# Two blocks of a weight matrix, fetched and converted among the first batch's squares

## The chip, the cores and the metric

The kernel runs on one core of a Trainium2 chip. The metric is the time of one execution in microseconds (us) of device time; lower is better. The engines named below are TensorE (PE, matrix products; PEld are its weight loads), VectorE (DVE), ScalarE (ACT), GpSimd (POOL) and SyncE (SP, which issues the DMA transfers). Each engine has its own sequence of instructions, written by the program, and waits where an operand isn't there yet.

## The reference

An attention over channels, followed by a gated two-layer network on all 24,320 tokens:

```
B, N, C = 4, 6080, 256;  d_ff = 2048
qn = q / (norm of q over the N tokens + 1e-6);  kn the same of k
s  = kn^T @ qn / tau              # [B, 256, 256]
a  = exp(s - s.max(-1));  a /= a.sum(-1) + 1e-9
x  = v @ a                        # [B, N, 256]
h  = x @ w_in                     # [B*N, 2048]
g  = h * sigmoid(1.702 * h)
out = g @ w_out                   # [B*N, 256]
```

q, k and v are float32; w_in and w_out are float64.

## The kernel before, in words

**What is computed where.** For each batch the kernel sums k^T q over the tokens into a 256 x 256 score matrix (TensorE), sums the squares of q and k for the norms, makes the softmax, and then folds the attention matrix into w_in: h = v @ (a @ w_in), so that the large work is one product of v with folded weights, a gate, and a product with w_out. The large products are done with operands split into a high and a low part (three matrix products for one), and by a seven-product scheme for 2 x 2 blocks (m1 to m7 in the listing). From about 71 us to the end TensorE does nothing but these; the loops there run over 4 batches, 6 chunks of tokens each, and 8 pairs of blocks of d_ff in each chunk.

**The float64 weights.** A block of w_in has 128 rows and 512 columns of float64 (512 KB). `win_fetch` loads it as pairs of 32-bit words, and `to_float32` makes float32 of it in two ScalarE steps (L132, L134) and four VectorE steps (L136, L138, L142, L147). `win_part` (L555, ScalarE) and `win_part_low` (L558, VectorE) then split the result into a high and a low part. The first two blocks (c = 0 and 1) make up the first group of columns; the first products of the folded weights (`weights_pair`, L602, tile ps_w) need both.

**The first batch.** `start_up` writes the instructions of the first batch's scores in program order. The 6080 tokens come in 25 units: units 0 to 23 are two groups of 128 tokens (the last of them one), unit 24 is the rest. For each unit `prepare` loads q and k, if the unit begins a load (units 1, 4, 7, 10, 13, 16, 19 begin one of 768 KB for q and one for k), squares both on ScalarE (L290, tile squares) and adds the squares to two running sums on VectorE (L293). `score` puts the unit's products on TensorE (L346, tile s), seven units behind `prepare`; a product of 128 x 256 stands in the trace as two passes. `add_both` (L298, L299) adds the two sums together. Behind the last unit stand, on SP's queue, the loads of w_in's first two blocks, w_out's first part, tau, v, and q and k of the next batch.

**The stretch that is planned.** What follows, to the end of the first 8 pairs, is put in order by `together`: it collects the instructions with estimated durations, and `arrange` places them engine by engine, with ready times for what is loaded or summed earlier (`late_at`; the token "acc" stands for the sum of squares). TensorE's row has a fixed order: the scores of units 18, 19 and 20, then `first_norms` (L451, tile ps_n, which needs the finished sum of squares), the scores of units 21 and 22, `first_spread` (L478, ps_b, which needs the norms' reciprocals from VectorE, L465 to L469, and diag from ScalarE), the scores of units 23 and 24, the transposes (L522), the folded weights (L602), then m5, m1, ... of the first pair (L719). Sixteen products for the next batch's scores (`score_first`, also L346) may be put between these from where the row stands at the transposes. ScalarE and VectorE get their order from the planner, so an instruction there that comes early can hold up what stands behind it.

The two blocks of w_in are among the planned work, behind the last square:

```
for c in range(NC2):
    state = win_convert(c, c)
    ...
    add("ACT", 0.62, ("win", 0, 0, c, 0), [("cv", "in", c, 5)], A.win_part, 0, c)
    add("DVE", 0.69, ("win", 0, 0, c, 1), [("win", 0, 0, c, 0)], A.win_part_low, c)
```

Of the kernel before, what the change touches and what calls it, by code (L numbers as in the profile page):

```python
# [28 lines left out]
def channel_attention_then_glu(  # L29
# [26 lines left out]
    NC2 = C // P  # L56
# [24 lines left out]
    cv = ctx.enter_context(tc.tile_pool(name="cv", bufs=2))  # L81
# [5 lines left out]
    def bank(tag, name):  # L87
        pool = {"a": ps_h, "b": ps_h, "c": ps_h, "s": ps_s}.get(tag, ps_o)
        return pool.tile([P, NCH], F32, tag=tag, name=name)
# [26 lines left out]
    def load_words(src, shape, pool=cv, tag="words"):  # L116
        raw = pool.tile([*shape, 2], U32, tag=tag, name="words")
        nc.sync.dma_start(raw, src)
        return raw
# [34 lines left out]
    win = {}  # L154

    def win_fetch(n):


        g, c = divmod(n, NC2)
        gs = slice(2 * g * GW, 2 * (g + 1) * GW)  # L160
        src = w_in[c * P : (c + 1) * P, gs].rearrange("p (f w) -> p f w", w=2)
        if g == 0:
            room = (sp, ("qs", "ks")[c])
        else:
            room = (wp, f"{('wh', 'wl')[c]}{g}")
        words["in", n] = load_words(src, [P, GW], *room)

    def win_convert(n, room=0):
        g, c = divmod(n, NC2)
        win[n] = sp.tile([P, GW], F32, tag=("raw_q", "raw_k")[c], name="win")  # L170
        yield from to_float32(win[n], words.pop(("in", n)), [P, GW], room)

    def wout_fetch(u):

        rows = w_out[2 * u * P : 2 * (u + 1) * P, :]
        src = rows.rearrange("(f p) (d w) -> p f d w", p=P, w=2)
        words["out", u] = load_words(src, [P, 2, C])
# [636 lines left out]
    def keep_warm():  # L814

        wide = gp.tile([P, NCH], F32, tag="g", name="wide", bufs=2)
        nc.vector.memset(wide, 1.0)
        ps = bank("b", "ps_y")
        for rhs in [ones] * 4 + [wide]:
            nc.tensor.matmul(ps[:, : rhs.shape[1]], lhsT=ones, rhs=rhs, start=True, stop=True)  # L820
# [3 lines left out]
    at, nxt = ats[:2]  # L824
# [2 lines left out]
    ready = []  # L827
    PAIRS = NF // 2

    def start_up():  # L830
        nc.scalar.activation(table, ones[:, 0:1], AF.Sqrt)
        keep_warm()
        for u in range(nu):
            ready.append(at.prepare(u))
            if u >= AHEAD:
                at.score(u - AHEAD, *ready[u - AHEAD])
        win_fetch(0)
        win_fetch(1)
        wout_fetch(0)
        nc.sync.dma_start(tau_sb, tau.partition_broadcast(P))  # L840
        v_load(0, 0, False)
        v_load(0, 0, True)
        nxt.fetched(0)
        nxt.fetched(2)
        win_fetch(2)
        win_fetch(3)
        at.add_both()
        wo.extend(wp.tile([P, NF, C], F32R, tag=f"wo_{n}", name=f"wo_{n}") for n in "hl")

    def first_softmax():  # L850

        A = at
        us = 1.0 / 0.68
        START = 36.4

        def add(eng, dur, token, deps, fn, *a):
            gather[0].append(Node(eng, dur * us, token, deps, fn, a))

        def score(u, *deps):
            dur = 0.86 if u == nu - 1 else 1.72  # L860
            add("PE", dur, ("s", u), deps, lambda: at.score(u, *ready[u]))

        def late_at(t, *tokens):
            for token in tokens:
                done(token, (t - START) * us)

        late_at(40.2, "acc")
        late_at(34.7, ("cv", "in", 0, "load"))
        late_at(36.0, ("cv", "in", 1, "load"))
        late_at(37.3, ("cv", "out", 0, "load"))  # L870
        late_at(41.5, "v1")
        late_at(44.8, "v2")
        late_at(47.5, ("raw", 1, 0))
        late_at(50.0, ("raw", 1, 1))
        late_at(51.4, ("cv", "in", 2, "load"))
        late_at(52.7, ("cv", "in", 3, "load"))
        add("SP", 0, ("cv", "out", 1, "load"), ["ns"], wout_fetch, 1)
        gather[0][-1].wait = 20.0

        s1 = nxt.score_first((2, 4, 6, 8, 10, 12, 14))  # L880
        score(nu - 7)
        score(nu - 6)
        score(nu - 5)
        add("PE", 0.65, "ns", ["acc"], A.first_norms)
        score(nu - 4)
        score(nu - 3)
        add("PE", 0.45, "nb", ["diag"], A.first_spread)
        score(nu - 2)
        score(nu - 1)
        for i in range(NC2):  # L890
            add("PE", 0.3, ("t", i), [("e", i)], A.transposes, i)
        for q in range(2):
            have = ["aTh", *(("win", 0, 0, c, 1) for c in range(NC2))]
            add("PE", 1.1 - 0.1 * q, ("w", 0, 0, q, "h"), have, A.weights_pair, 0, q, (0, 4))
            add("PE", 0.48, ("w", 0, 0, q), ["aTl"], A.weights_pair, 0, q, (4, 6))
        for n in range(8):
            add("PE", 0.86, ("s1", n), [("raw", 1, n // 4)], lambda: next(s1, None))
            gather[0][-1].flex = True

        add("ACT", 0.25, "root", ["ns"], A.first_root)  # L900
        add("DVE", 0.7, "turn", ["root"], A.first_turn)
        add("ACT", 0.5, "diag", ["turn"], A.first_diag)
        add("ACT", 0.4, "rq", ["nb"], A.first_rq)
        add("ACT", 1.5, "exp", ["root"], A.exp_table)
        for i in range(NC2):
            add("DVE", 0.9, ("x", i), ["rq", ("s", nu - 1)], A.softmax_a, i)
            add("ACT", 0.7, ("e", i), [("x", i), "exp"], A.softmax_b, i)
        add("DVE", 0.3, "z", [("e", 1)], A.softmax_c)
        add("ACT", 1.5, "table", ["aTh"], A.gelu_table)
        add("ACT", 0.59, "aTh", [("t", 1)], A.turned)  # L910
        add("DVE", 0.69, "aTl", ["aTh"], A.turned_low)

        for c in range(NC2):
            state = win_convert(c, c)
            key = ("cv", "in", c)
            for n, (eng, dur) in enumerate((("ACT", 0.6), ("ACT", 0.6), ("DVE", 0.42), ("DVE", 0.42), ("DVE", 0.67), ("DVE", 0.67))):
                add(eng, dur, (*key, n), [(*key, n - 1 if n else "load")], lambda s=state: next(s, None))
            add("ACT", 0.62, ("win", 0, 0, c, 0), [("cv", "in", c, 5)], A.win_part, 0, c)
            add("DVE", 0.69, ("win", 0, 0, c, 1), [("win", 0, 0, c, 0)], A.win_part_low, c)
        add("SP", 0, None, [("win", 0, 0, c, 1) for c in range(NC2)], A.win_keep, 0)  # L920

        V = ("v", 0, 0)
        for n in range(2):
            add("DVE", 0.69, (*V, "+", n), ["v1"], v_sum, 0, 0, False, n)
        for n in range(3):
            have = ["v2"] if n < 2 else [(*V, "+", 2), (*V, "+", 3)]
            add("DVE", 0.69, (*V, "+", 2 + n), have, v_sum, 0, 0, True, n)
        for tag, n, da, dd, have in (
            ("py", 0, 0.62, 0.69, [(*V, "+", 0)]),
            ("px", 0, 0.62, 0.69, ["v1"]),  # L930
            ("py", 1, 0.62, 0.69, [(*V, "+", 1)]),
            ("px", 1, 0.62, 0.69, ["v1"]),
            ("pz", 0, 0.62, 0.69, [(*V, "+", 2 + n) for n in range(3)]),
            ("pz", 1, 0.62, 0.69, [(*V, "+", 2 + n) for n in range(3)]),
            ("pw", None, 0.62, 0.69, [(*V, "+", 2 + n) for n in range(3)]),
        ):
            token = (*V, tag if n is None else f"{tag}{n}")
            add("ACT", da, (*token, 0), have, v_part, 0, 0, tag, n, False)
            add("DVE", dd, token, [(*token, 0)], v_part, 0, 0, tag, n, True)
        weight_ops(0, 0, gather[0])  # L940
# [15 lines left out]
    def done(token, t):  # L956
        if token is not None:
            ends[token] = t
# [49 lines left out]
    def arrange(nodes, row, ahead, near):  # L1008
# [1 line left out]
        ends = dict(begun_ends)  # L1010
        row = list(row)
        clock = dict.fromkeys(("PE", "ACT", "POOL", "SP"), 0.0)
        clock["ACT"], clock["DVE"] = 3.0, 5.6
        open_to = {e: [] for e in clock}
        users = {}
        unmet = {}
# [39 lines left out]
        while undone:  # L1056
            best = None
            for e in clock:
                at = list(choices(e))
# [19 lines left out]
            _, t, x = best  # L1079
# [27 lines left out]
    def together(n):  # L1107

        nodes = []
        gather.append(nodes)  # L1110
        first_softmax()
        for p in range(n):
            lay(p)
# [548 lines left out]
    for b in range(B):  # L1662
# [4 lines left out]
        if b + 1 < B:  # L1667
            o = b * NCHUNK * PAIRS
            u, last_u = ats[b + 1].direct, len(ats[b + 1].units)
# [57 lines left out]
```

## Time and profile before

| what | value |
|---|---|
| time, median of 3 runs | 2158.22 us (2157.47 to 2158.90) |
| span of the profiled execution | 2156.0 us |
| its own time beside its span | the profile gives the span alone; the median is 2.2 us above it |
| PE busy | 2148.4 us, 100% |
| ACT busy | 1552.9 us, 72% |
| DVE busy | 1278.0 us, 59% |
| POOL busy | 437.2 us, 20% |
| data moved by DMA | 153.5 MB, mean 71 GB/s |

The span runs from the first to the last instruction that the profiler saw; all starts below are counted from its beginning. Busy shares are means over stages with different limits: in the first 35 us the DMA engines are full, in the following 35 VectorE is, and then TensorE to the end. The duration of one instruction is from its start to its end; instructions of one engine overlap a little at their ends, so what a further one costs is the distance from start to start, which is shorter.

### The profile page before, as it was taken

Reading aid. Unit: us, or ns where it says so; the run is one execution under the profiler, and the core shown is the slowest. Engines: PE = TensorE matmul, PEld = TensorE weight load, DVE = VectorE, ACT = ScalarE, POOL = GpSimd, SP = SyncE. Lnnn points to the kernel's source line nnn. Section 1 sums busy time; section 2 is a strip of 40 time slices with the busy share of each in tenths; the row PEclk is TensorE's granted clock in tenths of the full one; section 3 lists DMA queues with packets and bytes.
Section 4 is the critical chain, followed back from the end, with each engine's and each line's share of the span. In section 5 each row is a group of like instructions: output and inputs, shape, how many; then the busy total and the mean of one; then the engine's idle time right before and its main releaser. Section 6 shows DMA issues by size and latency. Waiting matters only on the chain.

```text
span 2156.0 us, 26555 instructions
## 1 busy us (share of the span) xinstructions
PE 2148.4 (100%) x9720; PEld 1793.6 (83%) x9720; DVE 1278.0 (59%) x1925; ACT 1552.9 (72%) x2753; POOL 437.2 (20%) x457
## 2 busy tenths in 40 slices
PE   9999999999999999999999999999999999999999
PEld 8888888888888888888888888888888888888887
DVE  7986656655556565664555666566555545545443
ACT  7987777766777777776777777777676666666665
POOL 0003333230113342231012233223111200100100
PEclk9999999999999999999999999999999999999999
DMA  9433222221122121221113222122111110110100
GB/s 373 142 106 95 69 69 79 67 71 40 59 97 70 60 87 59 75 77 40 39 63 104 69 69 74 54 87 66 40 67 50 59 40 20 59 40 20 57 20 19
DMA packets 73843, 153.50 MB, mean 71 GB/s; under 512 B 6896, under 2 KB 14576, under 8 KB 73712
## 3 DMA queue, kind: packets, MB, share of 16 engines
q1 hardware_dynamic: 73712, 151.81, 21.2%
q8 instruction: 76, 1.25, 0.2%
q14 instruction: 55, 0.45, 0.1%
HBM read 122.68 MB, written 29.10 MB: 70 GB/s over the span
## 4 chain that ended last, share of the span: by engine, by line
PE 96%; DMA 2%; DVE 1%; ACT 0%; SPq 0%; issue 0%; DVEq 0%; ACTq 0%
PE ps_o L795 48%; PE ps_x L719 24%; PE ps_z L719 12%; PE ps_y L719 6%; PE s L385 4%; PE ps_w L584 2%; DMA raw<-in_k 1%; PE ps_w L602 0%; DMA v_raw<-in_vT 0%; DMA raw_k<-in_k 0%; DVE vl L701 0%; DVE v_raw L684 0%; SPq L263 0%; ACT vh L703 0%; PE ps_n L412 0%
## 5 line engine op out<-in xcount | busy, mean ns | idle before, releaser
L795 PE MATMUL ps_o<-gh,wo_l 128*128 128x512 f32 (+1 forms) x1536 | 594.9, 387 | 0.0
L795 PE MATMUL ps_o<-gh,wo_h 128*128 128x512 f32 (+1 forms) x1536 | 594.7, 387 | 0.0
L795 PE MATMUL ps_o<-gl,wo_h 128*128 128x512 f32 (+1 forms) x1536 | 470.6, 387 | 0.0
L782 DVE TENSOR_TENSOR gl<-g,gh 128x512 fp32r<-128x512 f32 (+1 forms) x384 | 274.6, 754 | 155.1 <-ACT gh L778 155.0
L330 POOL TENSOR_TENSOR acc<-acc,sq 128x256 f32<-128x256 f32 x276 | 228.1, 832 | 593.9 <-ACT sq L318 583.1
L782 DVE TENSOR_TENSOR gl<-ps_y,gh 128x512 fp32r<-128x512 f32 (+1 forms) x192 | 131.8, 686 | 348.8 <-ACT gh L778 348.4
L795 PEld LDWEIGHTS ps_o<-gh,wo_h 128*128 128x128 f32 x1536 | 288.3, 188 | 57.6
L795 PEld LDWEIGHTS ps_o<-gh,wo_l 128*128 128x128 f32 x1536 | 288.3, 188 | 57.5
L795 PEld LDWEIGHTS ps_o<-gl,wo_h 128*128 128x128 f32 x1536 | 288.3, 188 | 57.4
L719 PE MATMUL ps_x<-vh,wh 128*128 128x512 f32 (+1 forms) x768 | 299.6, 390 | 0.5 <-ACT g L773 0.2
L719 PE MATMUL ps_x<-vl,wh 128*128 128x512 f32 (+1 forms) x768 | 298.0, 388 | 0.0
L719 PE MATMUL ps_x<-vh,wl 128*128 128x512 f32 (+1 forms) x768 | 297.4, 387 | 0.0
L684 POOL TENSOR_TENSOR v_raw<-v_raw 128x512 f32<-128x512 f32 (+1 forms) x110 | 162.9, 1489 | 520.0 <-DMA v_raw<-in_vT 463.9
L773 ACT ACTIVATE r<-r 128x512 f32<-128x512 f32 (+1 forms) x192 | 120.6, 628 | 169.9 <-DVE r L762 169.9
L753 ACT COPY r<-ps_x 128x512 f32<-128x512 f32 (+1 forms) x189 | 110.3, 584 | 168.8 <-PE ps_x L719 168.4
L778 ACT CAST gh<-g 128x512 fp32r<-128x512 f32 (+1 forms) x384 | 216.2, 612 | 0.1
L782 DVE TENSOR_TENSOR gl<-r,gh 128x512 fp32r<-128x512 f32 (+1 forms) x192 | 150.7, 785 | 61.6 <-ACT gh L778 58.4
L719 PEld LDWEIGHTS ps_x<-vh,wh 128*128 128x128 f32 x768 | 144.4, 188 | 29.3 <-ACT g L773 1.6
L719 PEld LDWEIGHTS ps_x<-vh,wl 128*128 128x128 f32 x768 | 144.1, 188 | 28.9
L719 PEld LDWEIGHTS ps_x<-vl,wh 128*128 128x128 f32 x768 | 144.5, 188 | 25.4
L753 ACT COPY r<-ps_z 128x512 f32<-128x512 f32 (+1 forms) x192 | 112.2, 584 | 71.6 <-PE ps_z L719 70.5
L403 DVE TENSOR_TENSOR sums<-sums,s 128x256 f32<-128x256 f32 x138 | 57.9, 420 | 160.4 <-PE s L385 157.9
(137 smaller groups left out, 3263.9 us busy)
## 6 DMA issues: line engine op xcount, KB each, us to landing
v_raw<-in_vT SPq DMA_DIRECT2D x80, 512.0 KB, 4.2
out_T<-osb SPq DMA_DIRECT2D x80, 256.0 KB, 2.0
raw_q<-in_q SPq DMA_DIRECT2D x74, 256.0 KB, 2.6
raw_k<-in_k SPq DMA_DIRECT2D x74, 256.0 KB, 2.7
win_h<-win_h SPq DMA_DIRECT2D x16, 512.0 KB, 3.3
win_l<-win_l SPq DMA_DIRECT2D x16, 512.0 KB, 4.2
v_raw<-in_vT SPq DMA_DIRECT2D x16, 480.0 KB, 3.7
words<-in_w_in SPq DMA_DIRECT2D x8, 512.0 KB, 5.2
```

What stands on the lines that cost most here:

```text
L330: nc.gpsimd.tensor_tensor(acc, acc, sq[:, j, :], op=ALU.add)
L385: nc.tensor.matmul(out, lhsT=ks[:, j, low, ci], rhs=rhs, start=n == 0, stop=n == len(terms) - 1, skip_group_check=True,)
L403: nc.vector.tensor_tensor(out, out, part, op=ALU.add)
L584: nc.tensor.matmul(ps, lhsT=l[:, j, ci], rhs=r[:, j, :], start=n == 0, stop=n == 3 * NC2 - 1,)
L684: eng.tensor_tensor(out, a, z, op=ALU.subtract)
L719: nc.tensor.matmul(out, lhsT=l[:, wi, :], rhs=r[:, n, : self.hw], start=first and m == 0, stop=last and m == 2, skip_group_check=True,)
L753: nc.scalar.copy(r, getattr(self, src))
L773: nc.scalar.activation(g, source, AF.Gelu_apprx_sigmoid)
L778: nc.scalar.copy(gh, g)
L782: nc.vector.tensor_tensor(gl, g, gh.bitcast(F32), op=ALU.subtract)
L795: nc.tensor.matmul(out[d][:, : self.hw], lhsT=l[:, at_f, d * P : (d + 1) * P], rhs=r, start=first and l is wo[0] and r is gh, stop=last an ...
```

## The change

The loads of the two blocks are issued at units 10 and 13, behind those units' q and k, instead of behind the last unit. The eight steps of each block are written by `start_up`, two per unit: block 0 at units 13 to 16, block 1 at units 16 to 19. They are no longer part of the planned work, which gets a new ready time for the sum of squares (41.2 in place of 40.2) and for the split blocks.

```diff
+    FETCH = (10, 13)
+
+    def first_block(c):
+        yield from win_convert(c, c)
+        at.win_part(0, c)
+        yield
+        at.win_part_low(c)
+        yield
...
+        todo = [first_block(c) for c in range(NC2)]
         for u in range(nu):
             ready.append(at.prepare(u))
+            if u in FETCH:
+                win_fetch(FETCH.index(u))
+            for c in range(NC2):
+                for _ in range(2 if FETCH[c] + 2 < u <= FETCH[c] + 6 else 0):
+                    next(todo[c])
             if u >= AHEAD:
                 at.score(u - AHEAD, *ready[u - AHEAD])
-        win_fetch(0)
-        win_fetch(1)
         wout_fetch(0)
...
+    START, ACC = 36.4, 41.2
...
-        START = 36.4
...
-        late_at(40.2, "acc")
-        late_at(34.7, ("cv", "in", 0, "load"))
-        late_at(36.0, ("cv", "in", 1, "load"))
+        late_at(ACC, "acc")
+        for c in range(NC2):
+            late_at(START, ("cv", "in", c, 5), ("win", 0, 0, c, 1))
...
-        for c in range(NC2):
-            state = win_convert(c, c)
-            key = ("cv", "in", c)
-            for n, (eng, dur) in enumerate((("ACT", 0.6), ("ACT", 0.6), ("DVE", 0.42), ("DVE", 0.42), ("DVE", 0.67), ("DVE", 0.67))):
-                add(eng, dur, (*key, n), [(*key, n - 1 if n else "load")], lambda s=state: next(s, None))
-            add("ACT", 0.62, ("win", 0, 0, c, 0), [("cv", "in", c, 5)], A.win_part, 0, c)
-            add("DVE", 0.69, ("win", 0, 0, c, 1), [("win", 0, 0, c, 0)], A.win_part_low, c)
...
-        clock["ACT"], clock["DVE"] = 3.0, 5.6
+        clock["ACT"], clock["DVE"] = 3.0, (ACC - START) / 0.68
```

On ScalarE, among the squares of units 12 to 18 (tile squares; raw, raw_q and raw_k are loaded q and k; a plus marks a row that is new at its place, a minus one that is gone from it):

```order
-L290 ACTIVATE squares<-raw 128x512 x12
+L290 ACTIVATE squares<-raw 128x512 x8
+L132 ACTIVATE z<-words 128x512
+L134 ACTIVATE eighths<-words 128x512
+L290 ACTIVATE squares<-raw 128x512 x4
+L290 ACTIVATE squares<-raw_q 128x512
+L290 ACTIVATE squares<-raw_k 128x512
+L555 CAST win_h<-win 128x512
+L132 ACTIVATE z<-words 128x512
+L134 ACTIVATE eighths<-words 128x512
 L290 ACTIVATE squares<-raw_q 128x512
 L290 ACTIVATE squares<-raw_k 128x512
```

Block 0's L132 and L134 now stand between the squares of units 13 and 14, and its cast with block 1's pair between those of units 16 and 17; block 1's cast follows the squares of unit 19.

On VectorE, from the sum of unit 14 on (the rows L293 are the sums of one unit each):

```order
 L293 TENSOR_TENSOR sums<-sums,squares 128x1024
+L136 TENSOR_SCALAR z<-z 128x512
+L138 TENSOR_SCALAR z<-z 128x512
 L293 TENSOR_TENSOR squares<-squares 128x1024
+L142 SCALAR_TENSOR_TENSOR z<-words,z 128x512
+L147 ISA win<-z,eighths 128x1024
 L293 TENSOR_TENSOR sums<-sums,squares 128x1024
+L558 TENSOR_TENSOR win_l<-win,win_h 128x512
 L293 TENSOR_TENSOR squares<-squares 128x1024
+L136 TENSOR_SCALAR z<-z 128x512
+L138 TENSOR_SCALAR z<-z 128x512
 L293 TENSOR_TENSOR sums<-sums,squares 128x1024
```

Block 0's five steps stand between the sums of units 14 and 17; block 1's follow in the same manner between those of units 17 and 20. None stands behind the last sum any more.

On VectorE, behind the last sum (L298 and L299 finish the sum of squares; L684 and L701 work on v; L465 to L469 turn the norms into factors):

```order
 L298 TENSOR_TENSOR sums<-sums,squares 128x1024
 L299 TENSOR_TENSOR sums<-sums 128x2x256
-L136 TENSOR_SCALAR z<-z 128x512 x2
-L138 TENSOR_SCALAR z<-z 128x512 x2
-L142 SCALAR_TENSOR_TENSOR z<-words,z 128x512 x2
-L147 ISA win<-z,eighths 128x1024 x2
+L136 TENSOR_SCALAR z<-z 128x512
+L684 TENSOR_TENSOR v_raw<-v_raw 128x512 x2
 L465 RECIPROCAL rtau<-tau_sb 128x1
 L466 TENSOR_SCALAR rtau<-rtau 128x1
 L467 TENSOR_SCALAR rn<-rn 128x4
```

Between L469 and the softmax's first step (L492, tile x) there stood two L684, two L558, two L701 and one L136. There now stand one L701, L138, L142, three L684, L147 and two L701: work on v and on a block of w_out moves up to where the two blocks of w_in were.

On TensorE the norms keep their place behind unit 20. Of the next batch's products (L346, tile s), four passes that stood between the folded weights and m5 now stand behind m3 of the same pair; further on in the first pairs the folded weights of the second group stand a few products later.

## Rows read from the trace of the kernel before

**Rows 1.** The page's head and its part 1: busy time of each engine.
```profile
span 2156.0 us, 26555 instructions
...
PE 2148.4 (100%) x9720; PEld 1793.6 (83%) x9720; DVE 1278.0 (59%) x1925; ACT 1552.9 (72%) x2753; POOL 437.2 (20%) x457
```

**Rows 2.** Stretches of 5 us: busy time of each engine, TensorE clock, DMA share, GB/s.
```profile
25.00:30.00 5.00, 5.00 (x25) 4.40 (x24) 3.70 (x5) 3.70 (x8) 0.00 (x0) 1.00 1.01 420
...
35.00:40.00 5.00, 5.00 (x25) 4.41 (x24) 4.96 (x6) 4.70 (x11) 0.00 (x0) 1.00 0.82 290
...
45.00:50.00 5.00, 4.69 (x23) 3.80 (x22) 4.89 (x14) 4.28 (x9) 0.00 (x0) 1.00 1.03 419
...
65.00:70.00 5.00, 4.44 (x18) 3.01 (x18) 5.00 (x12) 4.98 (x11) 0.00 (x0) 1.00 0.24 97
```

**Rows 3.** Timeline (start, us, engine, line, operation): TensorE, 33 to 71 us.
```profile
33.20 8.80 PE L346 MATMUL s<-raw_q,raw_k 128*128 128x256 f32 x40
...
41.84 0.95 PE L451 MATMUL ps_n<-ones,sums 128*128 128x1 f32 x8
...
59.22 0.58 PE L719 MATMUL ps_z<-vh,wh 128*128 128x512 f32 x1
...
68.02 0.50 PE L719 MATMUL ps_z<-vh,wh 128*128 128x512 f32 x1 [0.36 <-ACT g L773]
...
71.09 0.39 PE L719 MATMUL ps_x<-vh,wh 128*128 128x512 f32 x1
```

**Rows 4.** Timeline of ScalarE and VectorE: the last squares and their sums, 24 to 42 us.
```profile
24.66 2.71 ACT L290 ACTIVATE squares<-raw 128x512 f32<-128x512 f32 x5 [0.42 <-DMA raw<-in_k]
25.32 1.22 DVE L293 TENSOR_TENSOR squares<-squares 128x1024 f32<-128x1024 f32 x1 [0.15 <-ACT squares L290]
...
29.30 0.63 ACT L290 ACTIVATE squares<-raw_k 128x512 f32<-128x512 f32 x1 [1.20 <-DMA raw_k<-in_k]
...
29.96 1.23 DVE L293 TENSOR_TENSOR sums<-sums,squares 128x1024 f32<-128x1024 f32 x1 [1.14 <-ACT squares L290]
...
31.10 1.22 DVE L293 TENSOR_TENSOR squares<-squares 128x1024 f32<-128x1024 f32 x1
...
33.70 1.23 DVE L293 TENSOR_TENSOR squares<-squares 128x1024 f32<-128x1024 f32 x1 [0.24 <-ACT squares L290]
...
40.82 0.69 DVE L299 TENSOR_TENSOR sums<-sums 128x512 f32<-128x512 f32 x1
```

**Rows 5.** Timeline of ScalarE and VectorE: the conversion of w_in's two blocks.
```profile
38.31 1.26 ACT L132 ACTIVATE z<-words 128x512 f32<-128x512 f32 x2 [0.30 <-DMA words<-in_w_in]
...
39.48 1.23 ACT L134 ACTIVATE eighths<-words 128x512 uint32<-128x512 uint32 x2
...
41.43 0.76 DVE L136 TENSOR_SCALAR z<-z 128x512 f32<-128x512 f32 x2
...
42.77 1.28 DVE L142 SCALAR_TENSOR_TENSOR z<-words,z 128x512 uint32<-128x512 uint32 x2
...
43.98 1.28 DVE L147 CUSTOM_DVE_ANT_0 win<-z,eighths 128x1024 uint16<-128x1024 uint16 x2
...
46.63 0.68 DVE L558 TENSOR_TENSOR win_l<-win,win_h 128x512 fp32r<-128x512 f32 x1
```

**Rows 6.** Timeline: the softmax's first step and the first product of the folded weights.
```profile
49.98 0.48 DVE L492 SCALAR_TENSOR_TENSOR x<-s,rn,rq 128x256 f32<-128x256 f32 x1
...
53.56 0.51 PE L602 MATMUL ps_w<-win_h,aT_h 128*128 128x256 f32 x2
```

**Rows 7.** Timeline of TensorE at the start of the program.
```profile
1.04 2.08 PE L820 MATMUL ps_y<-ones 128*128 128x128 f32 x8 [1.04 <-DVE ones L104]
...
2.91 1.74 PE L820 MATMUL ps_y<-wide,ones 128*128 128x512 f32 x2
...
4.49 1.89 PE L346 MATMUL s<-raw_q,raw_k 128*128 128x256 f32 x8
...
7.23 15.78 PE L346 MATMUL s<-raw_q,raw_k 128*128 128x256 f32 x72 [0.84 <-DMA raw_k<-in_k]
```

## The prediction, made before the changed kernel was run

> **What bounds the kernel now.** I read the page's busy times first. TensorE is busy for 2148.4 of 2156.0 us [rows 1], so a change that leaves its products alone, as this one does, can only move the few us in which it waits or is late, and 0.2% of the time (4.3 us) is about what a measurement can tell from no change.
>
> Second, the stretches of 5 us. From 25 to 30 us the DMA engines are full, at 420 GB/s, while VectorE is busy for 3.70 of 5 us; from 35 us on VectorE is at 4.89 to 5.00 of 5, and TensorE shows gaps from 45 to 70 [rows 2]. So the loads bound VectorE first, and VectorE then bounds TensorE up to about 71 us.
>
> Third, the timeline. TensorE runs the scores without a gap from 33.20 to about 41.85 and begins the norms at 41.84 [rows 3]. The sum of squares that these need is finished on VectorE at 40.82 + 0.69 = 41.51 [rows 4]. The two meet: there is no slack, and every us by which the sum of squares comes later is a wait of TensorE at its fixed place in the row. From 59.22 to 71.09 TensorE takes 11.87 us [rows 3] for 39 passes of the 512-wide kind and 4 of the next batch's scores. Twelve 512-wide passes take 71.09 - 68.02 = 3.07 with a wait in them; without one the pass takes close to 0.228 (I take that), a score pass 15.78 / 72 = 0.219 [rows 7]. That is 9.8 us of work, so 2.1 us are waits. These are the most the change can win there.
>
> **The moved loads.** Two transfers of 512 KB (0.524 MB) at 420 GB/s take 1.25 us each, in a stretch where the DMA engines are full [rows 2]. Block 0 goes ahead of unit 13's q and k, block 1 ahead of unit 16's. Unit 13's square of k, which waited for its transfer until 24.66, then starts at 25.91, and unit 16's at 29.30 + 2.5 = 31.80 [rows 4]. The scores don't notice: TensorE begins unit 16 at 33.20 [rows 3]. What was behind the last unit (w_out, v, the next batch) has the same bytes ahead of it as before, so it lands when it did.
>
> **The moved conversion.** Per block VectorE does L136, L138 (four in 42.77 - 41.43 = 1.34, so 0.335 each), L142 (two in 43.98 - 42.77, 0.605 each), L147 (0.60, its pair lasts as long as L142's) and L558, a two-input operation of the same size (0.60) [rows 5]: 2.48, and 4.95 for both. ScalarE does L132 and L134 (two L132 in 39.48 - 38.31: 0.585 each, L134 alike) [rows 5] and a cast at 0.52, the distance of its squares ((2.71 - 0.63) / 4) [rows 4].
>
> Where does VectorE have room? Between unit 13's sum and the end of the sums it takes 41.51 - 25.32 = 16.19, of which it waits 1.14 and 0.24 [rows 4]: 14.81 of work. After the change: unit 13's sum starts at 25.32 + 1.25 = 26.57, and 14.81 + 4.95 of work end at 46.3 if it never waits. It waits twice. ScalarE does block 0's pair between the squares of units 13 and 14, so unit 14's are done at about 28.7, one us after VectorE has finished unit 13 at 26.57 + 1.14 (distance 31.10 - 29.96) [rows 4] = 27.7. And unit 17's squares stand behind unit 16's (32.35), a cast, block 1's pair and themselves: 35.1, when VectorE is through with unit 16 and L558 at 34.65, 0.5 us. Block 0's first four steps lie in the time that unit 16's late data leave; nothing hides the rest. Sum of squares: 46.3 + 1.5 = 47.8, 6.3 us later. Bounds: 4.8 with no wait on VectorE, 7.3 with two more of 0.5.
>
> So TensorE stands for some 6.3 us in front of the norms. Nothing is queued that could fill this: its row is fixed there, and the next batch's products come later.
>
> **What comes back.** From the end of the sum to the softmax's first step VectorE takes 49.98 - 41.51 = 8.47 now [rows 4, 6], without a gap. Removed from in front of it are the two blocks (4.95); put there are three L684 and one L701 (0.60 each), L138, L142 and L147 (1.54): 3.94. Gain 1.0, so the softmax starts 47.8 + 7.5 = 55.3, 5.3 late. TensorE, restarted at 48, has its 16 passes of units 21 and 22, the spread and 8 passes of units 23 and 24 done by 54.8, before that. From there to the folded weights is a chain without slack, 3.58 us [rows 6], to 58.9. They took, with 12 passes of the next batch behind them, 59.22 - 53.56 = 5.66 [rows 3, 6]; now only 8 passes stand there (0.87 less), but VectorE has two more operations of 0.60 on v and w_out ahead of the attention matrix's low part, which costs TensorE about 0.25. m5 starts at 63.9 to 64.0, 4.75 late, with 4 passes (0.87) put off.
>
> Of the 2.1 us of waits from there on I take 1.8 as gone: VectorE has 5 us of work less, so what m6, m7, m4 and the next pair's m5 waited for is ready. Not all, because ScalarE's queue still releases m6 and m7. Bounds: 0 and 2.1. Sum: 4.75 + 0.87 - 1.8 = 3.8 us.
>
> **The clock after the wait.** What a wait of 6 us does to TensorE's clock no row shows; a wait of 0.84 before 7.23 left it at full pace. But the start shows the engine coming from idleness: 8 passes of 128 columns from 1.04 to 2.91 are 0.234 each, where 256 columns take 0.219 at full pace; so up to 4.65 it ran at half speed (1.2 of 2.4 GHz), though the clock's column reads 1.00 in every stretch of rows 2 [rows 7]. These 3.6 us cost 1.8. If the same happens at 48, the norms take a us more and the scores up to 51.5 twice their time; the scores of unit 24 then end at 56.5 instead of 54.8 and set the softmax, and the next batch's 12 passes delay the transposes: 1.6 us. Bounds 0 and 3.1 (twice as long at half speed). I take 1.6, as 6 us without work is more like the start than like 0.84.
>
> The Trainium skill, "TensorE: Matmul & The Clock Gate", Part 1 (the HAM clock gate), says that the array's clock falls to half when the engine has stood idle, and is full again only after sustained work. By that rule the sum is 5.4, without it 3.8.
>
> The sum by my forecast: 3.8 + 1.6 = 5.4 us slower. The span of 2156.0 becomes 2161.4; the median lies 2.2 above the span, so 2158.2 + 5.4 = 2163.6.
>
> **The rivals.**
> 1. *The clock holds.* For it: the wait before 7.23 cost nothing of the pace, and nothing in the trace gives the point from which one does. Then 3.8: 2162.0, inside 0.2%. Chance 0.30.
> 2. *The gaps take it all, not slower.* For it: VectorE waits more than it seems in the sums, 1.3 of 5 us from 25 to 30 [rows 2], and the late data make 2.5 us more. If the moved steps fitted there, the sum of squares would come only with the late data, 2.5 us late, and 1.0 + 2.1 would come back: 2157.6; if even these were hidden, at best 2155. It decides from the point at which VectorE's sum of unit 16 starts no later than its squares are ready. Against it: VectorE is busy for 4.96 of the 5 us from 35 to 40 [rows 2], and block 1's steps lie among these. Chance 0.07.
> 3. *The order doesn't fit the delay.* The planner thinks the sum of squares comes 1.0 later; if VectorE's and ScalarE's queues, with work on v and w_out moved up, hold up the first pair so that no wait goes (1.8) and the low clock lasts twice as long (1.5), it is 8.7: 2166.9. For it: 0.60 operations stand ahead of the attention's low part. Chance 0.10.
> 4. That the loads aren't early is excluded by the order; that something else in the dense part shifts by more than 1 us has 0.03 for either sign.
>
> **How the numbers follow.** My forecast, late sum and low clock, has 0.50. Of it, with the bounds on the sum of squares (-1.5 to +1.0), some four fifths lie above 4.3: 0.41; of rival 1 a third, 0.10; rival 3 all, 0.10; 0.02 from the rest: slower 0.63. Faster by over 0.2% needs more than all waits between 46 and 71 us: 0.02. No change: 0.35. The range of 8 in 10 goes from the clock holding with the smallest delay (3.8 - 1.5 = 2.3, 2160.5) to the forecast with half of rival 3's surplus and a us of delay (2166.0).
>
> **What would show it.** In the profile after: unit 16's square of k at 31.8 instead of 29.3; the sums without a gap from unit 17 on and ending at 47 to 49; the norms begun right behind with TensorE idle about 6 us before them, released by VectorE's L299; the passes of unit 21 at 0.43 each instead of 0.22 for the clock; the softmax's first step 5 to 7 us later; few waits between m5 and the second pair. If the norms start before 45, the step on VectorE's room is wrong; if they start at 48 and TensorE is dense again less than 2.5 us later than before, the step on what comes back is.

## The result, and the profile after

| | before | after |
|---|---|---|
| time, median of 5 runs | 2158.06 us (2157.32 to 2158.90) | 2169.63 us (2167.86 to 2170.44) |
| profiled execution, span | 2156.0 us | 2168.7 us (its own time 2170.44) |

The changed kernel is slower: ratio 1.0053, 95% interval 1.0043 to 1.0064, some 11.6 us. The profiled executions lie 12.7 us apart. The sign was forecast, the size was not: 5.4 us was the forecast, and 2166.0, some 8 us over before, the upper end of the range.

The page's head and part 1 of after answer to [rows 1]:

```profile
span 2168.7 us, 26548 instructions
...
PE 2152.6 (99%) x9720; PEld 1798.3 (83%) x9720; DVE 1279.6 (59%) x1925; ACT 1553.9 (72%) x2753; POOL 436.0 (20%) x457
```

TensorE does the same 9720 passes; 4.2 us of the 12.7 are more busy time of PE, and 8.5 us (12.7 - 4.2) are more idle time. So there are two kinds of loss, standing and going slowly. The stretches of 5 us say where (columns as in [rows 2]: stretch, busy us of PE, PEld, DVE, ACT, POOL, then the granted clock, DMA share, GB/s):

```profile
35.00:40.00 5.00, 5.00 (x25) 4.41 (x24) 3.82 (x6) 4.10 (x8) 0.00 (x0) 1.00 1.01 324
...
45.00:50.00 5.00, 0.00 (x0) 0.00 (x0) 4.93 (x7) 3.28 (x8) 0.00 (x0) 0.67 0.86 353
50.00:55.00 5.00, 4.89 (x16) 4.29 (x17) 4.53 (x12) 2.99 (x7) 0.00 (x0) 0.50 0.00 2
55.00:60.00 5.00, 5.00 (x20) 4.27 (x19) 3.17 (x6) 2.31 (x6) 0.00 (x0) 0.81 0.56 131
...
160.00:165.00 5.00, 3.68 (x17) 2.70 (x15) 2.79 (x6) 3.29 (x7) 0.00 (x0) 1.00 0.17 61
165.00:170.00 5.00, 4.16 (x11) 3.08 (x12) 4.38 (x7) 3.82 (x8) 1.43 (x2) 0.66 0.29 108
```

TensorE does nothing from 45 to 50 us; behind that its clock is at 0.50, the 1.2 GHz level. VectorE, full in before from 35 us on, is busy for 3.82 of 5 from 35 to 40, so part of the lateness is waiting. And there is a second hole, from 160 to 170 us, with another drop of the clock (0.66 from 165 to 170). Before has nothing like it:

```profile
160.00:165.00 5.00, 5.00 (x24) 4.14 (x23) 2.98 (x5) 3.88 (x9) 0.00 (x0) 1.00 0.68 216
165.00:170.00 5.00, 5.00 (x22) 3.75 (x22) 3.69 (x5) 4.24 (x8) 1.48 (x2) 1.00 0.69 243
```

The timeline of ScalarE and VectorE answers to [rows 4]; in brackets stands the idle time before the instruction and what ended it:

```profile
26.84 0.63 ACT L290 ACTIVATE squares<-raw 128x512 f32<-128x512 f32 x1 [2.14 <-DMA raw<-in_k]
27.51 1.22 DVE L293 TENSOR_TENSOR squares<-squares 128x1024 f32<-128x1024 f32 x1 [2.35 <-ACT squares L290]
29.69 1.23 DVE L293 TENSOR_TENSOR sums<-sums,squares 128x1024 f32<-128x1024 f32 x1 [0.96 <-ACT squares L290]
30.83 0.42 DVE L136 TENSOR_SCALAR z<-z 128x512 f32<-128x512 f32 x1
31.29 0.43 DVE L138 TENSOR_SCALAR z<-z 128x512 uint32<-128x512 uint32 x1
31.57 0.63 ACT L290 ACTIVATE squares<-raw_k 128x512 f32<-128x512 f32 x1 [0.35 <-DMA raw_k<-in_k]
...
34.21 0.62 ACT L555 CAST win_h<-win 128x512 fp32r<-128x512 f32 x1 [2.01 <-DVE win L147]
37.05 1.23 DVE L293 TENSOR_TENSOR squares<-squares 128x1024 f32<-128x1024 f32 x1 [1.14 <-ACT squares L290]
...
49.27 0.69 DVE L299 TENSOR_TENSOR sums<-sums 128x512 f32<-128x512 f32 x1
```

The sum of squares ends at 49.27 + 0.69 = 49.96 instead of 41.51. Unit 13's square of k waits for its data until 26.84. The cast of block 0 (L555) waits 2.01 us on ScalarE for VectorE's L147; the squares of unit 17 stand behind it, and VectorE then waits 1.14 us for these.

TensorE's timeline answers to [rows 3]:

```profile
50.11 1.83 PE L451 MATMUL ps_n<-ones,sums 128*128 128x1 f32 x8 [8.05 <-DVE sums L299]
51.80 3.76 PE L346 MATMUL s<-raw_q,raw_k 128*128 128x256 f32 x8
55.36 2.66 PE L346 MATMUL s<-raw 128*128 128x256 f32 x8
57.86 0.59 PE L478 MATMUL ps_b<-diag,ones 128*128 128x256 f32 x2
...
68.61 0.58 PE L719 MATMUL ps_z<-vh,wh 128*128 128x512 f32 x1
...
77.09 0.39 PE L719 MATMUL ps_z<-vh,wh 128*128 128x512 f32 x1
...
79.82 0.39 PE L719 MATMUL ps_x<-vh,wh 128*128 128x512 f32 x1
```

Eight passes of unit 21 take 55.36 - 51.80 = 3.56, 0.445 each, twice the 0.219 of full pace. In stretches of 1 us the granted clock is 0.50 up to 56 us, 0.54 from 56 to 57 and 1.00 behind that, so the low clock ends at about 57.0, 6.9 us behind the start of the norms. The first pair's m5 (68.61) is 9.39 late; the point that stood at 71.09 (now 79.82) is 8.73 late, so 0.7 us come back between them, and no wait stands there any more.

The second hole, in the timeline of all engines (SPq is SyncE's queue):

```profile
152.45 1.23 DVE L701 TENSOR_TENSOR vl<-v_raw,vh 128x1024 fp32r<-128x1024 f32 x1 [2.58 <-ACT vh L703]
...
153.70 2.13 SPq L669 DMA_DIRECT2D v_raw<-in_vT  x2
...
162.28 2.02 DVE L684 TENSOR_TENSOR v_raw<-v_raw 128x512 f32<-128x512 f32 x3 [2.09 <-DMA v_raw<-in_vT]
...
164.34 1.66 ACT L703 CAST vh<-v_raw 128x512 fp32r<-128x512 f32 x3 [0.27 <-DVE v_raw L684]
...
165.53 0.50 PE L719 MATMUL ps_x<-vh,wh 128*128 128x512 f32 x1 [1.85 <-ACT vh L703]
...
166.34 0.79 PE L719 MATMUL ps_x<-vl,wh 128*128 128x512 f32 x1 [0.31 <-DVE vl L701]
...
167.36 0.63 PE L719 MATMUL ps_z<-vh,wh 128*128 128x512 f32 x1
167.78 0.63 PE L719 MATMUL ps_z<-vl,wh 128*128 128x512 f32 x1
```

The second half of the next chunk's v is loaded from 153.70 on, VectorE waits for it until 162.28, ScalarE for VectorE, TensorE for both; then its 512-wide passes are 0.42 apart instead of 0.23. In before the first casts of that v stand at

```profile
129.90 1.07 ACT L703 CAST vh<-v_raw 128x1024 fp32r<-128x1024 f32 x1
...
148.16 0.62 ACT L703 CAST vh<-v_raw 128x512 fp32r<-128x512 f32 x1 [0.21 <-PE ps_x L719]
```

and in after the first half's at 151.37, 21.5 us later, and the second half's at 164.34, 16.2 later, though TensorE was only 8.6 us late there.

Why the load of the second half is late stands in the first two lines of that timeline: both halves use the same two buffers (the pool `cv`, bufs=2, tag words, in `v_load`), so the load has to wait until the first half's casts (L703) and low parts (L701) have read them. The first low part ends at 152.45 + 1.23 = 153.68, and the load begins at 153.70. SyncE's queue had stood 10.2 us for it; in before this wait was 1.0 us. So what moved is the first half's place in the order of VectorE and ScalarE, and the second half's load moved with it.

### The profile page after: what moved, and what is told of

It reads as the page before. It is cut to its first block, busy times and chain, and to the rows that moved or that the text cites. A ratio compares the mean times of both kernels' runs of the same rounds, so it can differ in the third digit from the quotient of the medians.

```text
span 2168.7 us, 26548 instructions
## 1 busy us (share of the span) xinstructions
PE 2152.6 (99%) x9720; PEld 1798.3 (83%) x9720; DVE 1279.6 (59%) x1925; ACT 1553.9 (72%) x2753; POOL 436.0 (20%) x457
## 3 DMA queue, kind: packets, MB, share of 16 engines
q8 instruction: 76, 1.25, 0.2%
## 4 chain that ended last, share of the span: by engine, by line
PE 97%; DMA 1%; DVE 1%; ACT 0%; issue 0%; SPq 0%; ACTq 0%
PE ps_o L795 48%; PE ps_x L719 24%; PE ps_z L719 12%; PE ps_y L719 6%; PE s L385 4%; PE ps_w L584 2%; PE s L346 1%; DMA raw<-in_k 1%; PE ps_w L602 1%; DMA raw_q<-in_q 0%; DMA v_raw<-in_vT 0%; DVE squares L293 0%; DVE vl L701 0%; DVE sums L293 0%; ACT squares L290 0%
## 5 line engine op out<-in xcount | busy, mean ns | idle before, releaser
L795 PEld LDWEIGHTS ps_o<-gh,wo_l 128*128 128x128 f32 x1536 | 288.5, 188 | 57.5
L684 POOL TENSOR_TENSOR v_raw<-v_raw 128x512 f32<-128x512 f32 (+1 forms) x110 | 163.8, 1498 | 518.8 <-DMA v_raw<-in_vT 371.5
L773 ACT ACTIVATE r<-r 128x512 f32<-128x512 f32 (+1 forms) x192 | 120.6, 628 | 167.4 <-DVE r L762 167.4
```

What stands on the lines that cost most here:

```text
L684: eng.tensor_tensor(out, a, z, op=ALU.subtract)
L773: nc.scalar.activation(g, source, AF.Gelu_apprx_sigmoid)
L795: nc.tensor.matmul(out[d][:, : self.hw], lhsT=l[:, at_f, d * P : (d + 1) * P], rhs=r, start=first and l is wo[0] and r is gh, stop=last an ...
```

## The experiments

The table shows by how much each kernel is later than before at five points (in before: end of the sum of squares 41.51, first m5 59.22, the m5 that stands at 149.32 and the one at 160.07, the span), and in the last column the median's distance from the median of before, run on the same chip. The points are those of one profiled execution each. From the column "at 149.32" to the column "at 160.07" is the price of the second hole; behind it hardly anything moves any more. The intervals of the ratios of after (1.0043 to 1.0064), e4, e5, e6 and e7 overlap, so a difference of 1 to 3 us between these kernels' times alone shows little; the readings below rest on the points.

| kernel | sum | first m5 | at 149.32 | at 160.07 | span | median |
|---|---|---|---|---|---|---|
| after | +8.45 | +9.39 | +8.60 | +12.45 | +12.7 | +11.6 |
| e1 loads only | +2.26 | +2.78 | +2.84 | +2.86 | +2.9 | +2.7 |
| e2 conversion only | +6.08 | +6.73 | +6.02 | +8.01 | +8.2 | +7.8 |
| e3 neither | -0.28 | -1.84 | -2.61 | +0.95 | +1.1 | +0.1 |
| e4 v earlier | +8.29 | +9.64 | +10.34 | +10.34 | +10.4 | +10.5 |
| e5 kept busy | +8.21 | +6.67 | +5.92 | +9.52 | +9.7 | +9.8 |
| e6 both | +8.66 | +7.61 | +8.37 | +8.40 | +8.4 | +8.5 |
| e7 cast later | +6.86 | +6.68 | +5.92 | +7.94 | +8.1 | +8.9 |
| e8 neither, v earlier | +0.73 | -0.32 | +0.42 | +0.39 | +0.5 | -0.1 |
| e9 planner told | +8.33 | +13.89 | +12.97 | +14.24 | +14.3 | +14.0 |

**e1: the loads alone.** The kernel before, with only the two loads moved.

```diff
             ready.append(at.prepare(u))
+            if u in (10, 13):
+                win_fetch((10, 13).index(u))
...
-        win_fetch(0)
-        win_fetch(1)
```

> The kernel before, with the two loads of w_in moved ahead of unit 13's and unit 16's q and k, and nothing else; the conversions stay planned, and the order on PE, DVE, ACT and POOL is that of before. Theory A (the late sum of squares is made by both parts, and the second wait by the new order of the planned stretch): the sum of squares ends 2.5 us late, at about 44, TensorE waits some 2.2 us in front of the norms, there is no wait near 165 us, and the time is 1 to 3 us above before (2159 to 2161). Rival C (the transfers alone make the sum late, the conversions are hidden): the sum ends at 49 to 50 and the time is 6 us or more above before.

Measured: 2160.69 us, ratio 1.0013 (1.0004 to 1.0023). TensorE's timeline:

```profile
43.92 1.02 PE L451 MATMUL ps_n<-ones,sums 128*128 128x1 f32 x8 [2.16 <-DVE sums L299]
44.81 3.51 PE L346 MATMUL s<-raw_q,raw_k 128*128 128x256 f32 x8
48.11 2.08 PE L346 MATMUL s<-raw 128*128 128x256 f32 x8
```

The late data alone cost 2.26 us of the sum. Behind a wait of 2.16 us the passes were slow (3.51 us for eight, with a granted clock of 0.66 from 45 to 50 us), and by the first m5 another 0.5 us was lost (2.78 - 2.26). There is no second hole.

**e2: the conversion alone.** The changed kernel without the two transfers; the blocks are filled with a constant.

```diff
+        for c in range(NC2):
+            words["in", c] = sp.tile([P, GW, 2], U32, tag=("qs", "ks")[c], name="words")
+            nc.gpsimd.memset(words["in", c].bitcast(F32), 1.0)
...
-            if u in FETCH:
-                win_fetch(FETCH.index(u))
```

> The changed kernel without the two transfers: GpSimd sets the two tiles to a constant at the start (so w_in's first group is not the real one), and the conversions run at their new place. Theory A: q and k land as before, VectorE still has 5 us more to do behind unit 13: the sum of squares ends at 46.5 to 47.5, TensorE waits 5 us, the clock falls, the wait near 165 us stays, 2165 to 2168. Rival C: the sum ends within 1 us of 41.5 and the time is that of before, or below.

Measured: 2165.78 us, ratio 1.0039 (1.0024 to 1.0054). The sum is 6.08 late. With the loads' 2.26 that makes 8.34, and both together measured 8.45: the two costs add up, and the steps did not hide behind the late data. The second hole is there, at a price of 1.99 us.

**e3: neither.** The changed kernel's order without the transfers and without the sixteen steps of the two blocks; the split blocks are constants.

```diff
     def first_block(c):
-        yield from win_convert(c, c)
-        at.win_part(0, c)
-        yield
-        at.win_part_low(c)
-        yield
+        for _ in range(8):
+            yield
```

> The changed kernel without the two transfers and without the sixteen steps: GpSimd writes a constant into both split tiles at the start (so w_in's first group is not the real one). The order of the planned stretch is that of the changed kernel. It shows what the change could give at best, and whether the second wait needs a late sum. Theory A: the sum ends at 41.5, the norms don't wait, the second pair's m5 comes 1 to 3 us earlier than before, but TensorE still waits about 2 us some 85 us behind the first m5, with the clock falling behind it: 2158 to 2161. Rival B (the second wait follows from the lateness): no second wait, 2155 to 2157.

Measured: 2158.08 us, ratio 1.0001 (0.9992 to 1.0011). Here the whole cost is taken away and the relief behind the sum is left. TensorE is 2.61 us ahead at the m5 of 149.32, and 0.95 late at that of 160.07:

```profile
153.95 0.51 PE L719 MATMUL ps_x<-vh,wh 128*128 128x512 f32 x1 [1.48 <-ACT vh L703]
154.76 0.50 PE L719 MATMUL ps_x<-vl,wh 128*128 128x512 f32 x1 [0.31 <-DVE vl L701]
```

So the second hole is no consequence of the late sum. It belongs to the planned order, and in this execution, in which the clock fell behind it (0.66 from 155 to 160 us), it cost 3.56 us, more than the relief gave. The ten times lie in two groups, five from 2157.4 to 2157.7 and five from 2158.5 to 2159.6 (the profiled one is 2158.93). The clock may have held in the first group; no profile shows it.

**e4: v earlier.** The changed kernel, whose planner has a goal that also counts how late the second half of the next chunk's v is.

```diff
-            return max(t + x.dur for _, t, x in plan if x.eng == "PE"), plan
+            end = max(t + x.dur for _, t, x in plan if x.eng == "PE")
+            at = [t + x.dur for _, t, x in plan if x.token and x.token in VLATE]
+            return end + 0.5 * max(0.0, (max(at) if len(at) == len(VLATE) else end + 20.0) - end + 0.0), plan
```

> The changed kernel, with the planner's goal extended: besides the end of TensorE's row it counts half of the time by which the last of the next chunk's v parts (px, py, pz) end behind it. The order it finds has the second half's casts of v in front of the ninth pair as in the kernel before. Theory A: the first wait stays (sum of squares at 50), the wait at 165 and the low clock behind it go, 3.9 us less than the changed kernel: 2165 to 2166.5. Rival B: the second wait stays and the time is 2168 to 2171.

Measured: 2168.45 us, ratio 1.0049 (1.0034 to 1.0064). The hole at 165 us is gone:

```profile
160.00:165.00 5.00, 4.79 (x22) 3.61 (x21) 3.63 (x6) 4.32 (x9) 0.00 (x0) 1.00 0.00 0
165.00:170.00 5.00, 5.00 (x24) 4.11 (x23) 4.25 (x7) 4.05 (x9) 1.44 (x2) 1.00 0.29 110
```

The first half's casts stand at 137.02 and 139.29 here, and no engine waits for the load. So the cause is v's place in the order; its load, its halving and its casts moved together and were not tried apart. But 1.74 us were paid earlier (10.34 late instead of 8.60 at 149.32), about half of it in waits from 70 to 80 us (PE 4.77 and 4.30 of 5, where after has 5.00). The time was 1.2 us below that of after, a third of what I expected.

**e5: TensorE kept busy in front of the norms.** The changed kernel with 17 products more.

```diff
+    def stay_warm():
+        ps = bank("b", "ps_y")
+        for _ in range(17):
+            nc.tensor.matmul(ps[:, :C], lhsT=ones, rhs=ready[20][0][:, 0, :], start=True, stop=True)
...
-        add("PE", 0.65, "ns", ["acc"], A.first_norms)
+        add("PE", 0.65, "ns", ["acc"], lambda: (stay_warm(), A.first_norms()))
```

> The changed kernel, with 17 further products of 128 x 256 (34 passes, some 7.4 us at full pace, results never read) put on TensorE ahead of the norms, where it stands for 8.05 us; nothing else differs in any engine's order. Theory (half clock is a term of its own, about 2.7 us at the softmax's first step): the sum of squares ends near 50.0 as before, the clock's column stays at 1.00 from 45 to 60 us, unit 21's passes take 0.22 each instead of 0.43 to 0.47, the softmax's first step comes near 57.5 instead of 60.22, and the time falls by about 2.5 us, to about 2167. The second wait near 165 us stays. Rival (the slow passes only fill time in which TensorE would wait for VectorE and ScalarE anyway): the passes are quick, the softmax's first step stays within 0.5 of 60.2, and the time stays at 2169 to 2170.

Measured: 2167.51 us (2165.93 to 2168.38), ratio 1.0043 (1.0029 to 1.0057). TensorE's timeline:

```profile
42.00 7.50 PE L866 MATMUL ps_y<-raw_q,ones 128*128 128x256 f32 x34
49.86 1.02 PE L451 MATMUL ps_n<-ones,sums 128*128 128x1 f32 x8 [0.37 <-DVE sums L299]
50.75 1.97 PE L346 MATMUL s<-raw_q,raw_k 128*128 128x256 f32 x8
```

Unit 21's passes are quick again, the softmax's first step comes at 57.5 instead of 60.22, as expected, and the first m5 at 65.89 instead of 68.61. The sum ended 0.24 earlier, so the half clock is worth 2.5 us by m5 (68.61 - 65.89 - 0.24). The second hole stays, at 3.60 us.

**e6: kept busy, and v earlier.** Both edits.

> The changed kernel with both: the 17 products ahead of the norms, and the planner's goal that takes the next chunk's second half of v forward. Theory: half clock and second wait are both gone, and what is left is the late sum of squares less what comes back: 8.45 - 2.2 = 6.2 us over the kernel before, about 2164.3, no stretch with the clock under 0.95 from 45 us on. Rival (the small waits from 70 to 80 us that the goal brought come from its order and not from the low clock): these stay, and the time is 2165.5 to 2167.

Measured: 2166.23 us, ratio 1.0038 (1.0025 to 1.0051). No second hole, and the clock at 1.00 in every stretch from 45 to 85 and 145 to 175 us, but 8.4 us late instead of 6.2: the rival was right. At the first m5 four more passes of the next batch stand ahead (0.9 us), and in the second pair TensorE waits 0.62 for ScalarE's L773. This order has waits of its own at the full clock too.

**e7: the cast one unit later.**

```diff
+        yield
+        yield
         at.win_part(0, c)
...
-                for _ in range(2 if FETCH[c] + 2 < u <= FETCH[c] + 6 else 0):
+                for _ in range(2 if FETCH[c] + 2 < u <= FETCH[c] + 7 else 0):
```

> The changed kernel with ScalarE's cast of each block, and VectorE's low part behind it, written one unit later (units 17 and 20 instead of 16 and 19); the planned stretch is the same. Theory (the cast, which waits for VectorE's L147, holds up the squares of unit 17 behind it and costs 1.1 us of the sum): ScalarE does unit 17's squares near 33.3 instead of 35.9, VectorE's sum of unit 17 starts without a wait near 35.2, the sum of squares ends at 48.8 instead of 49.96, and the time falls by about 1.1, to about 2168.5. Rival (VectorE only swaps one wait for another, as it is late data that sets it): the sum still ends at 49.7 to 50.0, and the time is unchanged.

Measured: 2166.57 us (2165.91 to 2168.69), ratio 1.0041 (1.0027 to 1.0056). Timeline of ScalarE and VectorE:

```profile
33.52 0.61 ACT L290 ACTIVATE squares<-raw_k 128x512 f32<-128x512 f32 x1
34.04 0.60 ACT L555 CAST win_h<-win 128x512 fp32r<-128x512 f32 x1
34.96 1.22 DVE L293 TENSOR_TENSOR squares<-squares 128x1024 f32<-128x1024 f32 x1
...
47.68 0.69 DVE L299 TENSOR_TENSOR sums<-sums 128x512 f32<-128x512 f32 x1
```

The wait in front of unit 17's sum is gone, and the sum ends at 48.37, 1.59 earlier (1.14 were expected; 0.28 of it was there already at unit 13's sum, which started at 27.23 instead of 27.51). The median was 3.1 us below that of after instead of 1.1. In this execution the rest is the clock: it was at 1.00 again from about 53.0 us on, 4.5 us behind the start of the norms, where after took 6.9, and unit 22's eight passes, from 53.42 on, took 1.89 us again; and it didn't fall in the second hole, which cost 2.02 us instead of 3.85.

**e8: neither, and v earlier.** e3 with the planner's goal of e4.

> The order of the changed kernel without the two blocks' loads and without their 16 steps (the first group of w_in is filled with a constant, so the first pair's h is not the reference's), now with the planner's goal for v. Theory (the second wait comes from the planned order alone, and what comes back is about 2.2 us): no wait near 160 us, the next pair's m5 at 65.9 as without the goal, and the time 1.5 to 2.2 us under the kernel before, about 2156. Rival (the goal's order brings waits of its own in the first pairs whatever the sum does): next pair's m5 at 66.5 or later, and a time of 2157 to 2158.5.

Measured: 2157.61 us, ratio 0.9999 (0.9990 to 1.0009). The second hole is gone, and so is the gain: TensorE waits in the first eight pairs (0.60 for L773 at 69.04, 0.40 for L758 at 108.62) and is 0.42 late at 149.32. The next pair's m5 comes at 67.58 (65.85 in e3) and the median lies between 2157 and 2158.5: the rival held. A part of the difference isn't the order's, though: the sum ended 0.73 late in this execution, where e3's ended 0.28 early. In neither of the two orders is moving this work worth anything that the times show, even when the work itself costs nothing.

**e9: the planner is told the true time.** The changed kernel with one number changed.

```diff
-    START, ACC = 36.4, 41.2
+    START, ACC = 36.4, 49.6
```

> The changed kernel, whose planner is told 49.6 us instead of 41.2 for the finished sum of squares (about where it really ends). Theory (what costs is the sum's lateness, the half clock behind it, and the next chunk's v, which this order too puts late): sum of squares near 50.0, norms behind a wait of 8 us, half clock to about 58, v's second half still late, time 2168 to 2170.5. Rival (the prediction's third: the order doesn't fit the delay, since the planner counts on a sum at 41.2): the time falls by 2.5 us or more, to 2167 or less, with fewer waits of VectorE between the sum and the first pair.

Measured: 2171.79 us, ratio 1.0064 (1.0048 to 1.0081); slower still (its four runs all lie above the five of after), and above my own range. Timeline of TensorE and VectorE:

```profile
47.78 5.05 PE L346 MATMUL s<-raw 128*128 128x256 f32 x12 [6.23 <-DMA raw<-in_k]
52.67 0.95 PE L451 MATMUL ps_n<-ones,sums 128*128 128x1 f32 x8
...
61.59 0.69 DVE L701 TENSOR_TENSOR vl<-v_raw,vh 128x512 fp32r<-128x512 f32 x1 [4.23 <-ACT vh L703]
```

The planner now put 12 passes of the next batch's scores into the gap in front of the norms. They waited 6.23 us for their data, started at 47.78, ran at the low clock (0.41 us each) and pushed the norms to 52.67, 2.8 us behind the finished sum; then VectorE waited 4.23 us for ScalarE's casts of v, and the softmax began at 64.2. So telling the planner the right time is no cure: here a truer ready time made a worse order.

One rival to all that is said here of orders was not tried. The planner searches with 400 random steps from a fixed seed (`SEED, ROUNDS = 3, 400`), and its goal is the end of TensorE's row alone. Each order is one draw of this search; how much of the second hole, and of e9's loss, another seed would give is open.

## Why the prediction was right in its sign and short in its size

Laid beside each other in us later than before, the prediction's terms and what the profiles of after and e5 show:

| step | predicted | measured |
|---|---|---|
| sum of squares | 6.3 | 8.45 |
| from the sum to the first m5, clock apart | -1.55 (4.75 - 6.3) | -1.54 (e5: 6.67 - 8.21) |
| half clock | 1.6 | 2.5 (9.39 - 8.45 + 1.54) |
| from m5 on: passes put off, waits gone | -0.9 (0.87 - 1.8) | -0.8 (8.60 - 9.39) |
| the dense part | 0 | 3.85 (12.45 - 8.60) |
| sum | 5.4 | 12.45 |

**Right.** What bounds the stretch, and how the delay goes through it: unit 16's square of k came at 31.57 (31.80 predicted), the norms were released by L299 behind a wait of 8.05 us, the passes behind them took twice their time, and the waits between the first m5 and the second pair went. "What comes back" is right to 0.1 us in both of its rows. In the first row that is in part luck: in e5 VectorE's way from the sum to the softmax gained 0.7 us (49.72 to 57.51 against 41.51 to 49.98; 1.0 predicted), and the way from there to m5 0.9 (0.55 predicted). The clock fell: the granted clock is 0.50 from 50 to 55 us, behind 8.05 us without work, and e5, where the gap is filled, has 1.00 there. The Trainium skill, "TensorE: Matmul & The Clock Gate", Part 1 (the HAM clock gate), says that the array's clock is at half after the engine has stood idle, and the trace agrees. The rival that the clock holds is refuted.

**Mis-sized: the sum of squares, "47.8, 6.3 us later".** It came 8.45 later, outside the prediction's own bounds of 4.8 to 7.3. Three things make the 2.15 us. First, unit 13's data: its sum starts at 27.51 where the step had 26.57, 0.94 more. It is 2.19 late, where I gave it one transfer's 1.25 (in e1 it is 1.65 late). Second, the steps: the rates came from [rows 5], where two blocks go side by side, 0.335 for L136 and 0.605 for L142. Now each step needs the one just in front of it, and L136 to L138 takes 31.29 - 30.83 = 0.46, L142 to L147 0.72 (32.76 to 33.48); where a step that doesn't need it follows, L136 takes 0.33 (49.88 to 50.21, L684). The whole comes to about 5.5 instead of 4.95 for both blocks, 0.6 more. Third, the waits: 0.96 and 1.14 instead of 1.0 and 0.5, as ScalarE's cast stood waiting for L147 with the next squares behind it. I had counted the cast's own time and not that it would wait; e7, with the cast moved, has no wait there. 0.94 + 0.6 + 0.6 = 2.1.

**Mis-sized: the clock.** 2.5 instead of 1.6, inside the bounds (0 to 3.1): the low clock lasted 6.9 us behind the start of the norms (50.11 to about 57.0), where I had 3.5 (48 to 51.5). Rival 3 had this half right, the low clock for twice as long; its other half, that no wait goes, did not come. With the late sum and the low clock together the softmax's first step came 10.2 us later (60.22), where "what would show it" had 5 to 7.

Two small things in the working: the start of the program isn't among the stretches of [rows 2], though the stretch from 0 to 5 us reads 1.00 as well; and the range's upper end, by its own words, is 5.4 + 1.65 + 1 = 8.05, so 2166.2 and not 2166.0.

**Failed: "that something else in the dense part shifts by more than 1 us has 0.03 for either sign".** This is the largest miss: the step put the dense part at nothing, and it measured 3.85 us. By itself it takes the forecast out of the range, whose upper end lies 7.8 over before (5.4 + 3.85 = 9.25); the two mis-sized terms alone make about 8.5, out of it too, but by less. I followed the planner's new order to the second pair and took what lies behind as given, because TensorE has no gap there in before. But the same plan also sets where the next chunk's v is loaded, halved and cast; that moved by about a pair, the second half's load stood 10.2 us for the buffers of the first half, and its consumer stands in a row without slack. e3 shows the hole without the late sum, e4 and e6 show it gone when v is put forward. Had the chance been given by what was known (a planned stretch of 100 us whose order is made anew), it would have had to be several times as large, and the range wider upward.

What stays open: why unit 13's data come 2.2 us late, not 1.25; it wasn't tried apart. Open too is whether another draw of the planner's search keeps the relief. A version better than before wasn't found; e3 and e8 show a relief of at most about 2.3 us (from -0.28 at the sum to -2.61 at 149.32 in e3), which both orders give back.

## What to carry to other kernels

Free time on an engine was worth nothing here to a step that enters the engine's queue in front of work with no slack: the cost was its full time, plus what waited behind it while it waited itself. Where a planner sets the order, read the new order to its end, and above all for each load whose consumer is in the bounding engine's row, and for the work that has to free its buffer; a change in the first 50 us made a hole at 165. And a wait of TensorE can cost more than its length: with what the clock took, 2.16 us cost 2.9 here, and 1.85 + 0.31 cost 3.85.

## What the runs showed of the hardware that I had not expected

The same wait may cost the clock or not. e5 and e7 reach the second hole by the same instructions at the same times (m5 at 155.24 in both, waits of 1.48 and 0.31). Windows of e5 from 160 us:

```profile
160.00:165.00 5.00, 3.21 (x11) 2.09 (x10) 4.13 (x8) 4.50 (x9) 0.90 (x2) 0.89 0.14 52
165.00:170.00 5.00, 5.00 (x18) 3.95 (x18) 3.60 (x7) 3.33 (x6) 0.52 (x1) 0.77 0.27 105
```

and of e7:

```profile
160.00:165.00 5.00, 3.21 (x13) 2.12 (x12) 3.73 (x7) 4.51 (x9) 0.90 (x2) 1.00 0.15 56
165.00:170.00 5.00, 5.00 (x23) 4.12 (x23) 4.65 (x9) 4.19 (x8) 0.54 (x1) 1.00 0.41 158
```

In e5 the clock fell, about 1.4 us after the engine had started again, and the hole cost 3.60 us; in e7 it held, and the hole cost 2.02. Behind the same two waits it also fell in e3 (3.56 us) and held in e2 (1.99 us). So either can follow on waits of 1.48 and 0.31 us, and two profiles of such kernels differ by some 1.6 us for that alone, which may be part of the spread of the runs of e5 and e7 (2.5 and 2.8 us).
